# The token sum of phi(k) in a gated mix of linear attention and SwiGLU: from one matmul with ones to a transposing DMA, a DVE sum and a row in DRAM

## The chip, the cores and the metric

The kernel runs on one core of a Trainium2 chip. The metric is the device time of one execution in microseconds (us). The engines of the core work side by side, each through its own list of instructions in order: PE (TensorE) does matmuls, DVE (VectorE), ACT (ScalarE) and POOL (GpSimd) do elementwise work and sums, and SP (SyncE) issues the transfers (DMAs). An instruction that needs a result of another engine or of a transfer waits for it, and everything behind it on its own engine waits too.

## The reference, cut to what matters

```python
def A(x, wqkv, wo):                      # S = 2048 tokens, D = 512, H = 32 heads of 16
    q, k, v = split(x @ wqkv)
    phi = lambda t: jnp.where(t > 0, t + 1, jnp.exp(t)) + 1e-6
    pq, pk = phi(q), phi(k)
    kv = einsum("bhsd,bhse->bhde", pk, v)
    z = einsum("bhsd->bhd", pk)          # the token sum of phi(k)
    num = einsum("bhqd,bhde->bhqe", pq, kv)
    den = einsum("bhqd,bhd->bhq", pq, z)[..., None] + 1e-6
    return (num / den) @ wo
def B(x, w1, w3, w2):                    # F = 1376
    return (silu(x @ w1) * (x @ w3)) @ w2
g = sigmoid((x * gate_w).sum(-1))
out = g * A(x) + (1 - g) * B(x)
```

The sum `z` has 512 numbers, 16 for each head. Every token needs all of them for its 32 denominators.

## The kernel before, in words

The 2048 tokens are 16 tiles of 128 (index `t`), or 4 blocks of 512 (index `tb`). The order of the instructions on each engine is the order in which the Python program writes them.

The **first part**, to about 46 us, loops over the 16 tiles. `q_step` and `k_step` project a tile (L167) and form phi on ACT and DVE (L180 to L185). `g_step` (L215) gathers the product of x and phi(k) in four PSUM banks. At the end of each `k_step`, POOL adds phi(k) into `zacc` (L199); the last tile's addition writes `zaccb` in bf16. `zaccb` then holds, in each of the 128 partitions, a partial sum for each of the 512 features. One matmul with a matrix of ones (L376) sums over the partitions and leaves the result in all 128 partitions at once, and DVE copies it to `zb` (L377).

The **second part** loops over the four blocks. For each of the ten slices `fc` of F, `glu_step` does four matmuls for the gate (L262), four for the up half (L268), silu on ACT (L273) and the product on DVE into `hT` (L274). The four PSUM banks of these are taken in turn by `mm_tile`, also by `rem_step`. In the first block, `kv_step` follows at fc 2, `m2_step` (L404 and L406 copy `M2`) at fc 4 and `rem_step(0)` at fc 7. `rem_step` computes the last 96 columns of F and the gate, and issues a transposing DMA (L252) that writes the eleventh slice of `hT`. After the ten slices, `out_step` does one output tile at a time: four matmuls with the weights `pqT` (L414), then eleven with the weights `hT` (L427), the last of which uses the slice that L252 brought.

The denominators go beside this, tile by tile. `den_products` multiplies pq by `zb` on POOL (`pr`, L281). `den_sums` sums the heads on DVE, adds 1e-6 and takes the reciprocal (L285, L288, L292). `den_scale` multiplies pq by it on POOL (`pqs`, L296) and issues a transposing DMA to `pqT` (L301). `den_step(t)` is `den_sums(t)`, `den_products(t + 1)` and `den_scale(t)`. Tiles 0 to 3 are done in the first block, at the slices that `den_at` names; the other twelve follow output tiles.

All transfers but one small load are issued by SP in the program's order. First come the loads; after them, as the work goes, the transposes to `pqT` and `hT` and the output writes.

Of the kernel before, what the change touches and what calls it, by code (L numbers as in the profile page):

```python
# [8 lines left out]
ACT = mybir.ActivationFunctionType  # L9
ALU = mybir.AluOpType  # L10
AX = mybir.AxisListType
FP32 = mybir.dt.float32
BF16 = mybir.dt.bfloat16
# [3 lines left out]
def kernel(  # L17
# [17 lines left out]
    nc = tc.nc  # L35
    P = nc.NUM_PARTITIONS

    Bb, S, D = A_x.shape
# [3 lines left out]
    KC = D // P  # L42
# [4 lines left out]
    FC = F // P  # L47
# [10 lines left out]
    w1_r = B_w1.rearrange("(kc d) f -> d kc f", d=P)  # L58
    w3_r = B_w3.rearrange("(kc d) f -> d kc f", d=P)

    consts = ctx.enter_context(tc.tile_pool(name="consts", bufs=1))
    work = ctx.enter_context(tc.tile_pool(name="work", bufs=2))
    psum = ctx.enter_context(tc.tile_pool(name="psum", bufs=1, space=bass.MemoryType.PSUM))
    ctx.enter_context(tc.manual_schedule())

    warm = nc.const_aps.tensor(1.0, [P, 256], BF16)
# [1 line left out]
    make_identity(nc, ident[:])  # L68


    ones = consts.tile([P, P], BF16, name="ones")
    nc.gpsimd.memset(ones[:], 1.0)
    bmask = consts.tile([P, HPC, Dh], BF16, name="bmask")
    nc.gpsimd.memset(bmask[:], 1.0)
    nc.gpsimd.affine_select(
        out=bmask[:], in_=bmask[:], pattern=[[-Dh, HPC], [0, Dh]], compare_op=ALU.is_ge,
# [3 lines left out]
        out=bmask[:], in_=bmask[:], pattern=[[Dh, HPC], [0, Dh]], compare_op=ALU.is_ge,  # L80
# [5 lines left out]
    zacc = consts.tile([P, D], FP32, name="zacc")  # L86
    zaccb = consts.tile([P, D], BF16, name="zaccb")
    zb = consts.tile([P, D], BF16, name="zb")

# [9 lines left out]
    w1 = consts.tile([P, KC, F0], BF16, name="w1")  # L101
    w3 = consts.tile([P, KC, F0], BF16, name="w3")
    w2 = consts.tile([P, FC + 1, D], BF16, name="w2")
    xT = consts.tile([P, KC, S], BF16, name="xT")
    act_pre = consts.tile([P, 1], BF16, name="act_pre")
    dq = nc.sync
# [5 lines left out]
    def load_wqk(kc):  # L112
        dq.dma_start(out=wqk[:, kc, :], in_=wqkv_r[:, kc, 0 : 2 * D])
# [6 lines left out]
    nc.scalar.dma_start(out=touch[:], in_=wqkv_r[:, 1:3, 0:16])  # L120
    for kc in range(KC):
        load_wqk(kc)
    natural = {3: (2, 4), 5: (4, 8), 7: (8, 12), 11: (12, 16)}
    for t in range(2, NT):
        load_xT(t)
        if t in natural:
# [2 lines left out]
    with nc.allow_non_contiguous_dma(reason="gate column"):  # L129
        dq.dma_start(  # L130
            out=wr[:, :, 2 * FR : NR], in_=gate_w.rearrange("(kc d o) -> d kc o", d=P, o=1)
        )
    dq.dma_start(out=wr[:, :, 0:FR], in_=w1_r[:, :, F0:F])
    dq.dma_start(out=wr[:, :, FR : 2 * FR], in_=w3_r[:, :, F0:F])
    for w, w_r, cuts in ((w1, w1_r, (0, KC)), (w3, w3_r, (0, 2, KC))):
        for a, b in zip(cuts, cuts[1:]):
            dq.dma_start(out=w[:, a:b, :], in_=w_r[:, a:b, 0:F0])
    dq.dma_start(out=wv[:], in_=wqkv_r[:, :, 2 * D : 3 * D])
    dq.dma_start(out=wo[:], in_=A_wo.rearrange("(kc d) n -> d kc n", d=P))
    w2_r = B_w2[0:F0, :].rearrange("(fc f) d -> f fc d", f=P)  # L140
    for a, b in ((0, 5), (5, FC)):
        dq.dma_start(out=w2[:, a:b, :], in_=w2_r[:, a:b, :])
    dq.dma_start(out=w2[:FR, FC, :], in_=B_w2[F0:F, :])

    pq = consts.tile([P, NT, D], BF16, name="pq")
# [11 lines left out]
    def mm_tile():  # L157
        turn["mm"] += 1
        return bank[4 + (turn["mm"] - 1) % 4]

    def ab_tile():
        turn["ab"] += 1
        return bank[(turn["ab"] - 1) % 4]
# [49 lines left out]
    def g_step(t, kcs=range(KC)):  # L213
        for kc in kcs:
            nc.tensor.matmul(  # L215
                bank[kc][:], lhsT=xN[:, t, kc * P : (kc + 1) * P], rhs=pk[t][:],
                start=(t == 0), stop=(t == NT - 1),
            )


    def rem_step(tb):

        hr = hrem[tb % 2]
        for half in range(2):
            ps = mm_tile()[:].rearrange("p (j n) -> p j n", j=2)
            for j in range(2):
                t = tb * TPB + half * 2 + j
                for kc in range(KC):
                    nc.tensor.matmul(  # L229
                        ps[:, j, 0:NR], lhsT=xT[:, kc, t * P : (t + 1) * P],  # L230
                        rhs=wr[:, kc, 0:NR], start=(kc == 0), stop=(kc == KC - 1),
                    )
            t0 = tb * TPB + half * 2
            sg = work.tile([P, 2, FR], BF16, tag="sgr", name="sgr")
            nc.scalar.activation(out=sg[:], in_=ps[:, :, 0:FR], func=ACT.Silu)
            nc.scalar.activation(
                out=th_all[:, t0 : t0 + 2], in_=ps[:, :, 2 * FR], func=ACT.Tanh, scale=0.5
            )
            nc.vector.tensor_tensor(
                out=hr[:, half * 2 : half * 2 + 2, 0:FR], in0=ps[:, :, FR : 2 * FR],  # L240
                in1=sg[:], op=ALU.mult,
            )
        tl = slice(tb * TPB, (tb + 1) * TPB)
        nc.vector.tensor_scalar(
            out=g_all[:, tl], in0=th_all[:, tl], scalar1=0.5, scalar2=0.5,
            op0=ALU.mult, op1=ALU.add,
        )
        nc.vector.tensor_scalar(
            out=omg_all[:, tl], in0=th_all[:, tl], scalar1=-0.5, scalar2=0.5,
            op0=ALU.mult, op1=ALU.add,  # L250
        )
        dq.dma_start(  # L252
            out=hT[tb][:, FC, :].rearrange("p (tt q) -> p tt q", q=P),
            in_=hr[:].rearrange("p tt f -> p (tt f)"), transpose=True,
        )

    def glu_step(tb, fc):
        fs = slice(fc * P, (fc + 1) * P)
        tok = slice(tb * TB, (tb + 1) * TB)
        g_ps = mm_tile()  # L260
        for kc in range(KC):
            nc.tensor.matmul(  # L262
                g_ps[:], lhsT=w1[:, kc, fs], rhs=xT[:, kc, tok],
                start=(kc == 0), stop=(kc == KC - 1),
            )
        u_ps = mm_tile()
        for kc in range(KC):
            nc.tensor.matmul(  # L268
                u_ps[:], lhsT=w3[:, kc, fs], rhs=xT[:, kc, tok],
                start=(kc == 0), stop=(kc == KC - 1),  # L270
            )
        sg = work.tile([P, TB], BF16, tag="sg", bufs=3, name="sg")
        nc.scalar.activation(out=sg[:], in_=g_ps[:], func=ACT.Silu)  # L273
        nc.vector.tensor_tensor(out=hT[tb][:, fc, :], in0=u_ps[:], in1=sg[:], op=ALU.mult)  # L274
# [4 lines left out]
    def den_products(t):  # L279
        pr[t] = work.tile([P, D], FP32, tag="pr", bufs=3, name="pr")  # L280
        nc.gpsimd.tensor_tensor(out=pr[t][:], in0=pq[:, t, :], in1=zb[:], op=ALU.mult)  # L281
# [21 lines left out]
    def den_step(t):  # L303

        den_sums(t)
        if t + 1 < NT:
            den_products(t + 1)
        den_scale(t)
# [61 lines left out]
    for t in range(2, NT):  # L370
# [1 line left out]
        if t + 2 < NT:  # L372
            k_step(t + 2)
        g_step(t)
    z_ps = mm_tile()
    nc.tensor.matmul(z_ps[:], lhsT=ones[:], rhs=zaccb[:], start=True, stop=True)  # L376
    nc.vector.tensor_copy(out=zb[:], in_=z_ps[:])  # L377
    for kc in range(KC):
        if kc % 2 == 0:
            nc.vector.tensor_copy(out=Gsb[:, kc, :], in_=bank[kc][:])  # L380
# [3 lines left out]
    def kv_step():  # L384
        kv_ps = ab_tile()[:].rearrange("p (c q) -> p c q", q=P)
        for c in range(KC):
            cs = slice(c * P, (c + 1) * P)
            for kc in range(KC):
                nc.tensor.matmul(  # L389
                    kv_ps[:, c, :], lhsT=wv[:, kc, cs], rhs=Gsb[:, kc, cs],  # L390
                    start=(kc == 0), stop=(kc == KC - 1),
                )
        nc.vector.tensor_tensor(
            out=kvT[:], in0=kv_ps,
            in1=bmask[:].rearrange("p h d -> p (h d)")[:, None, :].to_broadcast([P, KC, P]),
            op=ALU.mult,
        )

    def m2_step():
        for c in range(KC):  # L400
            ps = ab_tile()
            nc.tensor.matmul(ps[:], lhsT=kvT[:, c, :], rhs=wo[:, c, :], start=True, stop=True)  # L402
            if c % 2 == 0:
                nc.scalar.activation(out=M2[:, c, :], in_=ps[:], func=ACT.Copy)  # L404
            else:
                nc.vector.tensor_copy(out=M2[:, c, :], in_=ps[:])  # L406
# [36 lines left out]
                cs = slice(2 * P, D)  # L443
            dq.dma_start(out=rows[:, cs], in_=o[:, cs])

    den_products(0)
    den_at = {0: 0, 1: 1, 3: 2, 6: 3}
    for tb in range(NTB):
        for fc in range(FC):
            glu_step(tb, fc)  # L450
            if tb == 0:
                if fc in den_at:
                    den_step(den_at[fc])
                if fc == 2:
                    kv_step()
                if fc == 4:
                    m2_step()
                if fc == 7:
                    rem_step(0)
        for tt in range(TPB):  # L460
            out_step(tb, tt)
            if tb + 1 < NTB:
                if tt == 0:
                    hT[tb + 1] = work.tile([P, FC + 1, TB], BF16, tag="hT", name="hT")
                if tt == 1:
                    rem_step(tb + 1)
                den_step((tb + 1) * TPB + tt)
# [30 lines left out]
```

## Time and profile before

| | |
|---|---|
| median of 3 runs | 179.43 us (179.19 to 179.78) |
| the profiled execution | 179.22 us, its span 177.5 us |
| PE busy | 173.9 us (98%), 880 matmuls |
| DVE, ACT, POOL busy | 100.5, 62.3, 62.9 us |
| granted PE clock | 1.00 |
| transfers | 15.15 MB in 28940 packets |

The span is the time from the first to the last instruction that the profile shows. "SPq" rows are transfers as SP issues them; a transfer lands later than its row ends. "PEld" is the loading of a matmul's weights, which goes on beside the matmul before it. In the timeline a row stands for one instruction or for several alike (x4), with its start and its length in us; what stands in brackets is how long the engine was idle before it, and what ended that.

### The profile page before, as it was taken

What the parts mean: (1) busy time and instruction counts of PE and PEld (TensorE: products, weight loads), DVE (VectorE), ACT (ScalarE), POOL (GpSimd) and SP (SyncE); (2) the same over time, 40 slices, a digit from 0 to 9 for tenths busy, and PEclk for the clock granted to TensorE, in tenths of its full rate; (3) what the DMA queues carried; (4) which work ended last, traced back from release to release, by engine and by line L of the source; (5) the groups of instructions that cost most, each with busy time, mean ns of one, the idle gap of its engine ahead of it and who ended that gap; (6) DMA issues with size and microseconds to landing.
All of it is one profiled execution on the core that took longest, in us unless ns stands there. A gap on an engine that the chain in (4) does not pass through costs nothing.

```text
span 177.5 us, 2504 instructions
## 1 busy us (share of the span) xinstructions
PE 173.9 (98%) x880; PEld 84.1 (47%) x880; DVE 100.5 (57%) x195; ACT 62.3 (35%) x113; POOL 62.9 (35%) x105
## 2 busy tenths in 40 slices
PE   8999999999999999999999999999999999999993
PEld 5444444444454464644444464444445444444453
DVE  1399788888899663575434166634325664433222
ACT  3354544444735441332342223142322223342130
POOL 5086656656577240446200044540004432000000
PEclk9999999999999999999999999999999999999999
DMA  5989869994002120233100013520000342000001
GB/s 174 269 202 216 163 106 264 406 381 142 4 0 59 30 47 16 59 82 96 30 0 4 0 40 80 90 63 0 0 0 30 89 92 59 0 0 0 30 33 59
DMA packets 28940, 15.15 MB, mean 85 GB/s; under 512 B 20896, under 2 KB 27264, under 8 KB 28928
## 3 DMA queue, kind: packets, MB, share of 16 engines
q1 hardware_dynamic: 28656, 14.98, 32.3%
q8 instruction: 7, 0.11, 0.3%
q14 instruction: 5, 0.04, 0.1%
q10 hardware_dynamic: 272, 0.01, 0.1%
HBM read 8.43 MB, written 2.10 MB: 59 GB/s over the span
## 4 chain that ended last, share of the span: by engine, by line
PE 98%; DVE 0%; issue 0%
PE bank L427 21%; PE bank L262 19%; PE bank L268 19%; PE bank L167 16%; PE bank L414 8%; PE bank L215 8%; PE bank L229 3%; PE bank L315 2%; PE bank L389 1%; PE bank L402 0%; PE bank L321 0%; DVE o L431 0%; PE bank L376 0%
## 5 line engine op out<-in xcount | busy, mean ns | idle before, releaser
L274 DVE TENSOR_TENSOR hT<-bank,sg 128x512 bf16<-128x512 f32 x40 | 27.2, 681 | 30.9 <-PE bank L268 30.9
L268 PE MATMUL bank<-xT,w 128*128 128x512 bf16 x160 | 41.1, 379 | 0.0
L262 PE MATMUL bank<-xT,w 128*128 128x512 bf16 x160 | 41.1, 379 | 0.0
L427 PE MATMUL bank<-w,hT 128*128 128x512 bf16 (+3 forms) x198 | 40.7, 355 | 0.0
L273 ACT ACTIVATE sg<-bank 128x512 bf16<-128x512 f32 x40 | 23.9, 597 | 46.9 <-PE bank L262 46.9
L296 POOL TENSOR_TENSOR pqs<-pq,rden 128x512 bf16<-128x512 bf16 x16 | 16.9, 1055 | 65.1 <-issue 60.0
L167 PE MATMUL bank<-wqk,xT 128*128 128x512 bf16 x128 | 30.6, 382 | 0.0
L431 DVE SCALAR_TENSOR_TENSOR o<-bank,omg_all,aga 128x512 bf16<-128x512 f32 (+2 forms) x18 | 12.5, 692 | 28.1 <-PE bank L427 28.0
L427 PEld LDWEIGHTS <-hT 128*128 128x128 bf16 (+1 forms) x198 | 18.5, 98 | 19.8
L199 POOL TENSOR_TENSOR zacc<-zacc,pk 128x128 f32<-128x128 f32 x56 | 23.3, 446 | 10.4 <-DVE pk L185 10.4
L268 PEld LDWEIGHTS <-w 128*128 128x128 bf16 x160 | 15.7, 98 | 18.9
L262 PEld LDWEIGHTS <-w 128*128 128x128 bf16 x160 | 15.6, 98 | 18.5
L419 ACT ACTIVATE aga<-bank,g_all 128x512 f32<-128x512 f32 x16 | 11.0, 687 | 28.9 <-PE bank L414 28.9
L167 PEld LDWEIGHTS <-xT 128*128 128x128 bf16 x128 | 12.5, 98 | 15.0 <-issue 0.5
L281 POOL TENSOR_TENSOR pr<-pq,zb 128x512 f32<-128x512 bf16 x16 | 18.4, 1153 | 1.7 <-DVE zb L377 1.7
L414 PE MATMUL bank<-M,pqT 128*128 128x512 bf16 x64 | 16.4, 378 | 0.0
L215 PE MATMUL bank<-pk,xN 128*128 128x512 bf16 x64 | 16.4, 379 | 0.0
L180 ACT ACTIVATE eq<-bank 128x512 bf16<-128x512 f32 x16 | 9.4, 597 | 16.0 <-PE bank L167 16.0
L185 DVE SCALAR_TENSOR_TENSOR pk<-bank,emk 128x512 bf16<-128x512 f32 x16 | 11.1, 692 | 1.6
L180 ACT ACTIVATE ek<-bank 128x512 bf16<-128x512 f32 x16 | 9.4, 597 | 6.6 <-PE bank L167 6.6
L185 DVE SCALAR_TENSOR_TENSOR pq<-bank,emq 128x512 bf16<-128x512 f32 x16 | 11.1, 692 | 0.6
L285 DVE TENSOR_REDUCE den<-pr 128x32 f32<-128x512 f32 x16 | 10.8, 676 | 0.0
(50 smaller groups left out, 81.7 us busy)
## 6 DMA issues: line engine op xcount, KB each, us to landing
w<-in_B_w_dram SPq DMA_DIRECT2D x4, 640.0 KB, 9.6
out_dram<-o SPq DMA_DIRECT2D x15, 128.0 KB, 1.9
xN<-in_A_x_dram SPq DMA_DIRECT2D x3, 512.0 KB, 4.5
w<-in_B_w_dram SPq DMA_DIRECT2D x1, 1280.0 KB, 7.6
wqk<-in_A_wqkv_dram SPq DMA_DIRECT2D x4, 256.0 KB, 3.7
xN<-in_A_x_dram SPq DMA_DIRECT2D x2, 256.0 KB, 2.9
wv<-in_A_wqkv_dram SPq DMA_DIRECT2D x1, 512.0 KB, 10.7
wo<-in_A_wo_dram SPq DMA_DIRECT2D x1, 512.0 KB, 11.1
```

The lines of the kernel that those rows point to most:

```text
L167: nc.tensor.matmul(ps[:], lhsT=xT[:, kc, t * P : (t + 1) * P], rhs=w[:, kc, :], start=(kc == 0), stop=(kc == KC - 1),)
L180: nc.scalar.activation(out=e[:], in_=ps[:], func=ACT.Exp)
L185: nc.vector.scalar_tensor_tensor(out=dst, in0=ps[:], scalar=0.0, in1=em[:], op0=ALU.max, op1=ALU.add)
L199: nc.gpsimd.tensor_tensor(out=(zaccb if t == NT - 1 else zacc)[:, cs], in0=zacc[:, cs], in1=pk[t][:, cs], op=ALU.add,)
L215: nc.tensor.matmul(bank[kc][:], lhsT=xN[:, t, kc * P : (kc + 1) * P], rhs=pk[t][:], start=(t == 0), stop=(t == NT - 1),)
L262: nc.tensor.matmul(g_ps[:], lhsT=w1[:, kc, fs], rhs=xT[:, kc, tok], start=(kc == 0), stop=(kc == KC - 1),)
L268: nc.tensor.matmul(u_ps[:], lhsT=w3[:, kc, fs], rhs=xT[:, kc, tok], start=(kc == 0), stop=(kc == KC - 1),)
L273: nc.scalar.activation(out=sg[:], in_=g_ps[:], func=ACT.Silu)
L274: nc.vector.tensor_tensor(out=hT[tb][:, fc, :], in0=u_ps[:], in1=sg[:], op=ALU.mult)
L281: nc.gpsimd.tensor_tensor(out=pr[t][:], in0=pq[:, t, :], in1=zb[:], op=ALU.mult)
L414: nc.tensor.matmul(a_ps[:], lhsT=pqT[:, c, ts], rhs=M2[:, c, :], start=(c == 0), stop=(c == KC - 1),)
L427: nc.tensor.matmul(b_ps[:, 0:w], lhsT=hT[tb][:n, fc, tl], rhs=w2[:n, fc, cs], start=(fc == 0), stop=(fc == FC),)
```

## The change

The matmul with ones, the memset of `ones` and the DVE copy to `zb` go. In their place:

- a transposing DMA turns `zaccb` into `zaT` (feature chunks in the partitions, tokens along the row),
- `z_step` sums along the row on DVE (512 elements to 4 in each partition), casts to bf16, writes the 512 numbers to a row in DRAM (`zrow`) in 128 pieces of 8 bytes, and reads that row back into all 128 partitions (`zpk`),
- `z_order` puts the features of `zpk` into their right order on ACT and writes `zb`. It stands behind the two ACT copies of `m2_step` at fc 4, and the first `den_products` stands behind it,
- the den steps of tiles 0 to 3 move from the slices 0, 1, 3, 6 to the slices 5, 6, 7, 8,
- three loads are merged with their neighbours: tokens 8 to 15 of `xN`, `w3`, and `w2`.

At fc 7 the den step of tile 2 now stands in front of `rem_step(0)`. The instruction lists show these moves and no others; on PE the only instructions that differ are the weight load and the matmul of L376.

```diff
-    ones = consts.tile([P, P], BF16, name="ones")
-    nc.gpsimd.memset(ones[:], 1.0)
+    zpk = consts.tile([P, D], BF16, name="zpk")
+    zaT = consts.tile([P, KC, P], BF16, name="zaT")
+    zTb = consts.tile([P, KC], BF16, name="zTb")
+    zrow = dram.tile([1, D], BF16, name="zrow")
...
-    natural = {3: (2, 4), 5: (4, 8), 7: (8, 12), 11: (12, 16)}
+    natural = {3: (2, 4), 5: (4, 8), 8: (8, 16)}
...
-    for w, w_r, cuts in ((w1, w1_r, (0, KC)), (w3, w3_r, (0, 2, KC))):
+    for w, w_r, cuts in ((w1, w1_r, (0, KC)), (w3, w3_r, (0, KC))):
...
-    for a, b in ((0, 5), (5, FC)):
-        dq.dma_start(out=w2[:, a:b, :], in_=w2_r[:, a:b, :])
+    dq.dma_start(out=w2[:, 0:FC, :], in_=w2_r)
...
-    z_ps = mm_tile()
-    nc.tensor.matmul(z_ps[:], lhsT=ones[:], rhs=zaccb[:], start=True, stop=True)
-    nc.vector.tensor_copy(out=zb[:], in_=z_ps[:])
+    dq.dma_start(out=zaT[:], in_=zaccb[:], transpose=True)
+
+    def z_step():
+        zT = work.tile([P, KC], FP32, tag="zT", bufs=1, name="zT")
+        nc.vector.tensor_reduce(out=zT[:], in_=zaT[:], op=ALU.add, axis=AX.X)
+        nc.vector.tensor_copy(out=zTb[:], in_=zT[:])
+        dq.dma_start(out=zrow[0, :].rearrange("(p kc) -> p kc", kc=KC), in_=zTb[:])
+        dq.dma_start(out=zpk[:], in_=zrow[0:1, :].to_broadcast([P, D]))
+
+    def z_order():
+        nc.scalar.activation(
+            out=zb[:].rearrange("p (kc q) -> p kc q", q=P),
+            in_=zpk[:].rearrange("p (q kc) -> p kc q", kc=KC), func=ACT.Copy,
+        )
...
-    den_products(0)
-    den_at = {0: 0, 1: 1, 3: 2, 6: 3}
+    z_step()
+    den_at = {5: 0, 6: 1, 7: 2, 8: 3}
...
                 if fc == 4:
                     m2_step()
+                    z_order()
+                    den_products(0)
                 if fc == 7:
                     rem_step(0)
```

More of the change, by code (lines that the diff above doesn't have):

```diff
@@ L63 @@
     psum = ctx.enter_context(tc.tile_pool(name="psum", bufs=1, space=bass.MemoryType.PSUM))
+    dram = ctx.enter_context(tc.tile_pool(name="dram", bufs=1, space=bass.MemoryType.DRAM))
     ctx.enter_context(tc.manual_schedule())
```

## The prediction, made before the changed kernel had run

> **What bounds the kernel now.** I read the page from the top: busy shares, then the chain that ended last.
>
> ```profile
> PE 173.9 (98%) x880; PEld 84.1 (47%) x880; DVE 100.5 (57%) x195; ACT 62.3 (35%) x113; POOL 62.9 (35%) x105
> ...
> PE 98%; DVE 0%; issue 0%
> ```
>
> PE is busy from end to end and carries 98% of the chain; only the time before its first matmul and after its last one is not PE. So a saving counts only if it takes matmuls off PE, and an addition costs only if PE comes to wait for it. DVE, ACT and POOL have room on average; what matters is when their results arrive.
>
> Next the chain cut to the place of the change, start and duration in us:
>
> ```profile
> 45.53 0.86 PE bank L215 x4
> 46.39 0.24 PE bank L376
> 46.63 0.86 PE bank L262 x4
> 47.49 0.86 PE bank L268 x4
> ```
>
> L376 is the token sum of phi(k), one matmul with a slot of 0.24 us. PE does not stand still for it: the last piece of `zaccb` ends on POOL at 44.50 + 1.70 = 46.20, before the slot begins. Afterwards the glu groups (L262 gate, L268 up) follow each other every 0.86 us.
>
> Then the timeline, for what the four early den steps do today and what comes next on each engine (start, duration, engine, line, operation):
>
> ```profile
> 44.50 1.70 POOL L199 TENSOR_TENSOR zaccb<-zacc,pk 128x128 bf16<-128x128 f32 x4 [1.12 <-DVE pk L185]
> ...
> 47.13 0.68 DVE L377 CAST zb<-bank 128x512 bf16<-128x512 f32 x1
> ...
> 47.89 2.27 POOL L281 TENSOR_TENSOR pr<-pq,zb 128x512 f32<-128x512 bf16 x2 [1.69 <-DVE zb L377]
> ...
> 49.08 0.69 DVE L274 TENSOR_TENSOR hT<-bank,sg 128x512 bf16<-128x512 f32 x1
> ...
> 56.41 1.09 ACT L404 ACTIVATE M<-bank 128x512 bf16<-128x512 f32 x2 [0.48 <-PE bank L402]
> ...
> 58.86 0.69 DVE L274 TENSOR_TENSOR hT<-bank,sg 128x512 bf16<-128x512 f32 x1 [0.54 <-PE bank L268]
> ...
> 64.97 1.22 SPq L252 DMA_TRANSPOSE hT<-hrem  x1
> ...
> 67.47 2.26 PEld L427 LDWEIGHTS <-hT 128*128 128x128 bf16 x11
> ```
>
> The last two rows are the ones that decide. L252 moves the remainder block of `hT`; it is issued at 64.97 and lands 2.4 us later, at 67.4. It is the weights of the eleventh L427 matmul of the first output tile. The eleven weight loads begin at 67.47, one each 0.216 us, so the eleventh begins at 67.47 + 10 x 0.216 = 69.63: 2.2 us of room before the change.
>
> **What is removed.** The matmul: 0.24 us of PE, all of it on the path. Everything after it on PE, where nothing else is late, moves 0.24 earlier; I subtract that below. The `zb` cast (0.68 on DVE) goes too, off the path. So does the memset of `ones` on POOL, at the start, where POOL waits 5.7 us for the first pk. With `z_ps` gone the four glu banks turn by one place: the second gate-up pair now uses banks of q(14) and q(15), the latter freed by DVE at 46.52 + 0.69 = 47.21 and wanted at about 48.8. No cost.
>
> **The merged loads.** Tokens 8 to 15 of xN come in one 1 MB transfer, the w3 and w2 loads become one each. The bytes are the same. xT(9) is the first with more ahead of it, 512 KB; at the 202 to 269 GB/s of the second and third slice that is 2.0 to 2.6 us. It is issued near 14.0, landed within 4.8 us at worst, and its k projection runs at 25.7, so the cover is 6.9 us; without it the cost would be up to those 2.6 us on PE. The w2 load is needed at 67 and the traffic of all loads ends near 41, before and after. Zero, from 0 to +0.2.
>
> **The new chain to `zpk`.** The transposing DMA follows `zaccb` on SP, whose loads are all issued by 38: issue 46.22. The SBUF-to-SBUF transposes (pqT, L301) land in 2.4 us at the median and 3.2 at the worst, so 48.62. DVE has by then ended the two Gsb casts (47.21 + 1.28 = 48.5). The 512-element reduce costs the 0.68 of the den reduce, the 128x4 cast 0.16 (row of omg_all): done at about 49.5. Behind these two on DVE stands the first hT multiply (49.08 before); it now runs 49.54 to 50.23. Who waits for that is the third up group, which reuses its bank: 50.78 - 0.24 = 50.54. So the wait is hidden with 0.3 us to spare; a landing of 3.2 would cost 0.5. The next hT starts earlier than before, since the den sums are no longer between.
>
> The row write of 128 pieces of 8 bytes has no equal in the trace. Above stands the gate column (1 KB in 2-byte pieces) at 2.8 and the touch load (32-byte pieces) at 2.9; below the 64 KB output write at 1.5; the worst output write is 3.7. I take 2.9, the small-piece rows being nearest. The read by all partitions, 1 KB each: from 2.6 (the 96 KB wr loads) to 4.8 (worst xN); I take 2.8. Issued at 49.6, that makes 52.5 and 55.3. SP waits twice, and behind it stand only the pqT transposes, which have nothing to move yet.
>
> The Trainium skill's page "DMA: Bandwidth & Descriptors" (Specifications) speaks against this step: transfers under 512 bytes are done by read-modify-write. Its section "Anatomy of one DMA", a fit for another issuing path, puts 2.0 us plus bytes over 436 GB/s on each, which as an estimate makes 2.0 and 2.3 us and ends the chain at 53.9 in place of 55.3; the sum would be the same by both, as the next step does not start before 57.
>
> **ACT copy and the late den steps.** `z_order` stands on ACT behind the two M2 copies: 57.50 - 0.24 = 57.26. So the chain above has 2.0 us of cover. I give the copy 0.60 (ACT rows of 128x512: 0.54 to 0.69), to 57.86. The sg activation behind it (57.92 - 0.24 = 57.68 before) starts 0.2 late, and its hT multiply, which waits for PE until 58.62, does not notice.
>
> From here the order is POOL: pr0, pr1, scale0, pr2, scale1, pr3, scale2. pr0 and pr1 take 2.27, from 57.94 to 60.21. DVE does hT(5) to 58.86 + 0.69 - 0.24 = 59.31, then sums0: 1.28 (reduce start to reciprocal end, as at 61.19 to 62.47), to 60.59; 0.09 on to POOL. Now POOL is the limit: scale0 1.06, pr2 1.15, scale1 1.06, pr3 1.15, scale2 1.06 from 60.68: 5.48, to 66.16. DVE's sums1 and sums2 (about 62.4 and 64.2) are ready before POOL asks.
>
> SP then issues pqT(2) at 66.18, and only behind it the hT remainder, since `den_step` stands ahead of `rem_step` at fc 7: 1.28 us later (63.69 to 64.97 in the trace), 67.46. It lands 2.4 us on, at 69.86. PE wants it at 69.63 - 0.24 = 69.39. So PE waits 0.47 us in the first output tile. Before the change this room was 2.2 us; it is used up by moving four den steps behind the glu steps that follow M2.
>
> Other readers: pqT(0) lands at about 64.2 for 66.4, pqT(1) at 66.4 for 69.6, pqT(2) at 68.6 for 74.3, pqT(3) at 71 for 77.4. The first remainder multiply on DVE goes from 63.33 to behind sums2 and ends near 64.7 (hT(6), sums1, hT(7), sums2 one after another); the bank that it frees is asked for at 65.10 - 0.24 = 64.86, so 0.1 to 0.2 us of cover, and a wait there would put off PE's need of the hT remainder by as much, so the two do not add. From the fourth output tile on all is as before.
>
> **The sum.** -0.24 + 0.47 = +0.23 us. The profiled execution took 179.22 (span 177.5 and 1.7 around it), so 179.45; the median of the runs is 0.21 above the profiled one, so 179.6 (179.66, of which I take the lower side, since a weight load of 98 ns has a slot of 216 and so some 0.1 us in hand). A measurement of this kernel can tell about 0.3%, 0.54 us, from no change. So: no measurable change.
>
> **Rivals.**
> - *Nothing is late.* If the POOL chain is half a microsecond quicker, or the reduce is, PE keeps the whole 0.24: 179.2. For it: many of these rows overlap by 0.03 to 0.1. Against: seven steps in series have to give it. Also inside 0.3%. A gain above 0.54 has no place in the chain, as no more PE work leaves; it would need a shift in the kernel's start or end that I can't see.
> - *Slower: the trip through DRAM decides.* ACT waits for `zpk` with M2 done. This begins when the read lands after 57.26, that is when write and read take over 7.6 us together. With the worst rows, 3.7 + 4.8, it lands at 58.1, 0.84 late; 0.14 is hidden under hT(5) and 0.7 goes one for one into the hT remainder: +0.9, 180.35. Each microsecond more costs one more. For it: piece size and the write-then-read pair are outside the trace. Against: even 2-byte pieces under full load took 2.8.
> - *Slower: the first hT is late.* The transposing DMA lands at 3.2 instead of 2.4: third up group 0.5 late, +0.7, 180.15. Against: 15 of 16 pqT landings are 2.4 or 2.5.
> - *The change does less than it says:* the merged loads delay a projection before 46 us, up to +2.6 with the cover gone. Against: 6.9 us of cover.
>
> **How the numbers follow.** My sum with its stall between nothing and 0.75 (so a net of -0.24 to +0.5, the first rival included): 0.65, all within 0.3%. The DRAM trip or a POOL chain longer than I have it: 0.18; the late first hT: 0.08; loads: 0.04; together 0.30 slower. Faster by over 0.3%: 0.05, unexplained. The range runs from 179.0 (first rival less the scatter of the runs, 0.2) to 180.6 (DRAM rival plus the same); what is left out is a DRAM trip over 8.8 us, delayed loads and an unexplained gain.
>
> **What would show it.** Right: no L376 on PE; zaT landing near 48.6, zpk by 56; ACT's copy starting near 57.3 behind M2 and not behind a DMA; hT remainder issued near 67.5; the idle time of PE's eleventh L427 weight load in the first output tile at 0.2 to 0.6 us, released by the hT DMA. Wrong: idle time on ACT before the copy, on PE at the third L268 group, or before 46 us.

## The result and the profile after

| | before | changed |
|---|---|---|
| median | 179.44 us (179.12 to 179.78, 6 runs) | 181.05 us (180.68 to 181.28, 6 runs) |
| ratio, 95% interval | | 1.0079 (1.0063 to 1.0095) |
| profiled execution | 179.22 us, span 177.5 | 180.97 us, span 179.3 |

The changed kernel is slower by 0.8%, 1.1 to 1.7 us by the interval. The page of the changed kernel shows PE at the same work (one weight load fewer; 16 of its matmul records are missing) and the chain no longer on PE alone:

```profile
PE 173.4 (97%) x863; PEld 84.1 (47%) x879; DVE 101.7 (57%) x196; ACT 62.6 (35%) x114; POOL 62.8 (35%) x104
...
PE 93%; DVE 4%; issue 1%; DVEq 0%
```

The 4% of DVE lie almost all in one place, from 59 to 67 us. This is the chain of the changed kernel at the end of it (start, duration, what):

```profile
64.29 0.60 DVE den L287
...
64.92 1.12 DVE den L290
...
66.33 0.30 DVE hrem L241
66.64 0.04 issue
66.68 1.02 PE bank L264 x4
```

The timeline there, with POOL beside DVE. In `den_sums`, L287 is the sum over the heads, L290 the addition of 1e-6 (128x32) and L294 the reciprocal; on POOL, L283 is the product of `den_products` and L298 the scaling of `den_scale`; L241 is the remainder multiply in `rem_step`, L246 a step of the gate behind it:

```profile
58.39 2.26 POOL L283 TENSOR_TENSOR pr<-pq,zb 128x512 f32<-128x512 bf16 x2 [11.70 <-ACT zb L389]
...
60.44 0.25 DVE L290 TENSOR_SCALAR den<-den 128x32 f32<-128x32 f32 x1
...
61.54 0.67 DVE L287 TENSOR_REDUCE den<-pr 128x32 f32<-128x512 f32 x1
...
62.17 1.15 POOL L283 TENSOR_TENSOR pr<-pq,zb 128x512 f32<-128x512 bf16 x1
...
62.25 1.11 DVE L290 TENSOR_SCALAR den<-den 128x32 f32<-128x32 f32 x1
...
63.40 0.35 DVE L294 RECIPROCAL rden<-den 128x32 f32<-128x32 f32 x1
...
64.84 1.15 POOL L283 TENSOR_TENSOR pr<-pq,zb 128x512 f32<-128x512 bf16 x1
64.92 1.11 DVE L290 TENSOR_SCALAR den<-den 128x32 f32<-128x32 f32 x1
...
66.33 0.56 DVE L241 TENSOR_TENSOR hrem<-bank,sgr 128x192 bf16<-128x192 f32 x2
66.50 1.05 POOL L298 TENSOR_TENSOR pqs<-pq,rden 128x512 bf16<-128x512 bf16 x1 [0.51 <-DVE rden L294]
66.68 1.02 PE L264 MATMUL bank<-xT,w 128*128 128x512 bf16 x4 [1.16 <-DVE hrem L241]
...
66.81 0.77 DVE L246 TENSOR_SCALAR g_all<-th_all 128x4 f32<-128x4 f32 x1
...
68.87 0.18 DVE L290 TENSOR_SCALAR den<-den 128x32 f32<-128x32 f32 x1
```

An addition that takes 0.18 us alone takes 1.11 when a product of POOL has just begun, and ends 0.04 us after the product. This happens in tiles 1 and 2, so the remainder multiply (L241) runs late, the PSUM bank that it frees is late, and the first gate matmul of fc 9 waits for it: 1.54 us from the matmul before it in place of 0.22. In the kernel before, the same group starts without a wait:

```profile
65.10 1.03 PE L262 MATMUL bank<-xT,w 128*128 128x512 bf16 x4
```

The hold lasts as long as what is left of POOL's instruction. Tile 0's addition met the last 0.2 us of its two products (58.39 + 2.26 = 60.65) and took 0.25; L246, of the same form (TENSOR_SCALAR), met a scaling and took 0.77. All four end 0.03 to 0.04 us after POOL's instruction.

The profiled execution is 1.75 us longer. Three terms are read from the two timelines. The first is the start: the first gate weights of fc 0 are loaded at 46.52 in place of 46.26, although the matmul of 0.24 us in front of them is gone, so the part up to there took 0.50 longer. The second is the stretch from there to the end of the last matmul: 129.77 in place of 128.46, +1.31. The third is the end, from the last matmul to the end of the span: 2.96 in place of 2.78, +0.18.

### The profile page after: what moved, and what is told of

Same layout as the page of the kernel before. It is cut to its first block, busy times and chain, and to the rows that moved or that the text cites. A ratio compares the mean times of both kernels' runs of the same rounds, so it can differ in the third digit from the quotient of the medians.

```text
span 179.3 us, 2489 instructions
## 1 busy us (share of the span) xinstructions
PE 173.4 (97%) x863; PEld 84.1 (47%) x879; DVE 101.7 (57%) x196; ACT 62.6 (35%) x114; POOL 62.8 (35%) x104
## 4 chain that ended last, share of the span: by engine, by line
PE 93%; DVE 4%; issue 1%; DVEq 0%
PE bank L443 21%; PE bank L264 18%; PE bank L270 17%; PE bank L169 16%; PE bank L217 8%; PE bank L430 8%; PE bank L231 2%; PE bank L317 2%; DVE den L290 1%; DVE hT L276 1%; DVE den L287 1%; PE bank L405 0%; PE bank L418 0%; PE bank L323 0%; DVE o L447 0%
## 5 line engine op out<-in xcount | busy, mean ns | idle before, releaser
L264 PE MATMUL bank<-xT,w 128*128 128x512 bf16 x158 | 40.9, 379 | 1.4 <-DVE hrem L241 1.2
L443 PE MATMUL bank<-w,hT 128*128 128x512 bf16 (+4 forms) x197 | 40.6, 355 | 0.1
L270 PE MATMUL bank<-xT,w 128*128 128x512 bf16 x154 | 40.3, 379 | 0.2
L298 POOL TENSOR_TENSOR pqs<-pq,rden 128x512 bf16<-128x512 bf16 x16 | 16.9, 1055 | 56.1 <-issue 50.8
L283 POOL TENSOR_TENSOR pr<-pq,zb 128x512 f32<-128x512 bf16 x16 | 18.4, 1153 | 11.7 <-ACT zb L389 11.7
L287 DVE TENSOR_REDUCE den<-pr 128x32 f32<-128x512 f32 x16 | 10.8, 676 | 0.0
```

Of the source, the lines that this page charges most:

```text
L264: nc.tensor.matmul(g_ps[:], lhsT=w1[:, kc, fs], rhs=xT[:, kc, tok], start=(kc == 0), stop=(kc == KC - 1),)
L270: nc.tensor.matmul(u_ps[:], lhsT=w3[:, kc, fs], rhs=xT[:, kc, tok], start=(kc == 0), stop=(kc == KC - 1),)
L443: nc.tensor.matmul(b_ps[:, 0:w], lhsT=hT[tb][:n, fc, tl], rhs=w2[:n, fc, cs], start=(fc == 0), stop=(fc == FC),)
```

## The experiments

Theory 1: the addition stands still beside POOL, makes the bank late, and PE waits. Theory 2: the den steps are late in themselves, through the trip to DRAM or the chain of products on POOL. "Stretch" and "end" below are the second and third term above, from each kernel's profile, to about 0.01 us; ratios are to the kernel before, run on the same chip. The rows come from several chips, so two medians alone do not compare.

| | median us | ratio (95%) | fc 0 weights at | stretch | end |
|---|---|---|---|---|---|
| before (profile of 179.22) | 179.44 | | 46.26 | 128.46 | 2.78 |
| changed | 181.05 | 1.0079 (1.0063 to 1.0095) | 46.52 | 129.77 | 2.96 |
| e1 changed again | 181.01 | 1.0077 (1.0063 to 1.0092) | 46.57 | 129.78 | 2.97 |
| e2 no add | 179.45 | 1.0004 (0.9989 to 1.0018) | 46.64 | 128.46 | 2.99 |
| e3 remainder first | 179.67 | 0.9999 (0.9984 to 1.0015) | 46.76 | 128.46 | 2.99 |
| e4 late den alone | 180.98 | 1.0071 (1.0051 to 1.0091) | 46.55 | 129.71 | 2.77 |
| e5 reduce for add | 179.65 | 0.9991 (0.9972 to 1.0009) | 46.94 | 128.56 | 2.97 |
| e6 extra ACT | 180.06 | 1.0013 (0.9995 to 1.0032) | 46.94 | 128.46 | 2.97 |
| e7 merged loads alone | 179.63 | 0.9997 (0.9980 to 1.0015) | 46.52 | 128.47 | 2.98 |
| e8 remainder first, POOL copy | 179.51 | 0.9974 (0.9955 to 0.9993) | 46.55 | 128.46 | 2.79 |
| e11 tiles 2, 3 at fc 8, 9, POOL copy | 179.19 | 0.9986 (0.9971 to 1.0001) | 45.92 | 128.46 | 2.78 |
| e12 before, no add | 179.67 | 1.0011 (0.9994 to 1.0028) | 46.70 | 128.46 | 2.79 |

**e1, the changed kernel again.** No edit.

> The changed kernel unaltered, in another call. Two things made up the +1.75 us of its profile: PE waits 1.3 us for a bank at the ninth slice's successor (gate matmuls of fc 9), and everything before 46 us is 0.5 us late because the PE clock was granted at 5.97 us of the span in place of 5.00. If the grant falls by chance, this run's profile has another grant time and the front moves with it, half a us per us, and the middle (fc 9) still has its 1.3 us. If the merged loads or the new tiles cause the late front, the grant is again near 5.9 to 6.0 and the time 181.0.

The time and the wait at fc 9 came back (1.53 us between matmuls). The start was late again, but not as I had it: the clock record begins with full grant at 4.94 us, 1.03 earlier than in the first profile, and the first gate weights still came at 46.57. Here the slow first matmuls are short, 1.26 us for four, and PE instead lost about half a microsecond waiting at 6.8 and 7.5 us, which is when the third and fourth wqk loads landed (issued near 2.2 and 2.7, 4.6 and 4.8 us under way). So the start varies for at least two reasons. This run alone does not show that the change has no part in it; the kernels of e4, e6, e7 and e12, which keep the old token sum, have the first gate weights at 46.52 to 46.94.

**e2, without the addition.**

```diff
-        nc.vector.tensor_scalar(out=den[:], in0=den[:], scalar1=1e-6, scalar2=None, op0=ALU.add)
```

> Leaves out the addition of 1e-6 in den_sums (all 16 tiles). Theory 1 (that addition, a DVE tensor_scalar, stands still while a POOL product runs: 1.11 us in place of 0.18 for tiles 1 and 2, which makes the remainder multiply late and with it the bank of fc 9): den sums take 1.0 to 1.1 us, PE's wait at fc 9 is gone, the hT remainder may then be waited for by up to 0.47 us; 0.9 to 1.3 us less than the changed kernel, 179.8 to 180.2. Theory 2 (the den steps are too late in themselves, POOL's chain of products sets the end): POOL's chain is as long as before, at most 0.3 us less, 180.7 to 181.0.

The stretch is that of the kernel before to 0.01 us, and the time falls 1.6. Theory 2 said 0.3 at most. The late hT remainder shows in the weight loads of this run, where the eleventh waits for its transfer:

```profile
68.08 1.82 PEld L440 LDWEIGHTS <-hT 128*128 128x128 bf16 x9
70.09 0.10 PEld L440 LDWEIGHTS <-hT 96*128 96x128 bf16 x1 [0.19 <-DMA hT<-hrem]
70.24 0.75 PEld L427 LDWEIGHTS <-pqT 128*128 128x128 bf16 x4
```

The loads behind it are back in step at 70.24: PE lost nothing.

**e3, remainder first.**

```diff
+                if fc == 7:
+                    rem_step(0)
                 if fc in den_at:
                     den_step(den_at[fc])
...
-                if fc == 7:
-                    rem_step(0)
```

> The changed kernel with rem_step(0) ahead of den_step(2) at fc 7. Theory 1: the remainder multiplies run before sums2, the bank of fc 9 is free in time and the hT remainder is issued near 65; the collisions stay and now delay hT(8) and hT(9): hT(9) ends near 69.9, 0.2 us after PE wants its weights. 0.8 to 1.2 us less than the changed kernel, 179.9 to 180.3. Theory 2 (the chain through DRAM and POOL is what PE waits for): no difference, 181.0.

The direction is theory 1's, the size was missed: PE has no wait at all. The additions are as slow as before in tiles 1 and 3 (1.11; tile 2's took 0.43), and hT(9) ends at 69.87, when its weights are asked for near 69.9.

**e4, the late den steps alone**, with the matmul for the token sum and without any of the new transfers.

```diff
-    den_products(0)
-    den_at = {0: 0, 1: 1, 3: 2, 6: 3}
+    den_at = {5: 0, 6: 1, 7: 2, 8: 3}
...
                     m2_step()
+                    den_products(0)
```

> The kernel before, with its matmul for the token sum and its loads, but den_products(0) behind m2_step and den steps 0 to 3 at fc 5 to 8. Theory 1: the adds of tiles 1 and 2 collide with POOL's products as in the changed kernel, PE waits at fc 9 for 0.6 to 1.3 us: 180.1 to 180.8. Rival (the new chain with its transfers is the cause): 179.4, no wait of PE at fc 9.

This one edit costs what the whole change costs. Its timeline has the same two rows and the same wait, with `zb` ready since 48 us:

```profile
62.13 1.16 POOL L281 TENSOR_TENSOR pr<-pq,zb 128x512 f32<-128x512 bf16 x1
62.20 1.12 DVE L288 TENSOR_SCALAR den<-den 128x32 f32<-128x32 f32 x1
...
64.80 1.15 POOL L281 TENSOR_TENSOR pr<-pq,zb 128x512 f32<-128x512 bf16 x1
64.88 1.11 DVE L288 TENSOR_SCALAR den<-den 128x32 f32<-128x32 f32 x1
...
66.64 1.02 PE L262 MATMUL bank<-xT,w 128*128 128x512 bf16 x4 [1.09 <-DVE hrem L239]
```

**e5, another operation in the addition's place.**

```diff
-        nc.vector.tensor_scalar(out=den[:], in0=den[:], scalar1=1e-6, scalar2=None, op0=ALU.add)
+        den2 = work.tile([P, H], FP32, tag="den2", name="den2")
+        nc.vector.tensor_reduce(
+            out=den2[:], in_=den[:].rearrange("p (h d) -> p h d", d=1), op=ALU.add, axis=AX.X
+        )
...
-        nc.vector.reciprocal(out=rden[t][:], in_=den[:])
+        nc.vector.reciprocal(out=rden[t][:], in_=den2[:])
```

> The changed kernel with the addition of 1e-6 (left out) replaced by a DVE tensor_reduce over one element, of the same 128x32 size: as many DVE instructions and as much DVE work as in the changed kernel, but an operation whose rows never stretched beside POOL (den reduce 0.67 to 0.69 everywhere). Theory 1 (only the tensor_scalar form stands still beside POOL): the replacement takes about 0.2 us in tiles 1 and 2, PE's wait at fc 9 is 0 to 0.4 us, 179.5 to 179.9. Rival (any third DVE instruction there, or a wait of it for the reduce's result, takes 1.1 us): as the changed kernel, 181.0.

The replacement (L291) takes 0.18 and 0.19 in tiles 1 and 2 with an instruction of POOL in flight, a product and a scaling:

```profile
62.60 0.18 DVE L291 TENSOR_REDUCE den<-den 128x32 f32<-128x32 f32 x1
...
64.44 0.19 DVE L291 TENSOR_REDUCE den<-den 128x32 f32<-128x32 f32 x1
```

```profile
62.53 1.15 POOL L283 TENSOR_TENSOR pr<-pq,zb 128x512 f32<-128x512 bf16 x1
63.64 1.06 POOL L299 TENSOR_TENSOR pqs<-pq,rden 128x512 bf16<-128x512 bf16 x1
```

So it is the form of the instruction, and not a third DVE instruction at that place. The Trainium skill's page "SBUF — State Buffer" (Who interferes with whom) states this rule: a tensor_scalar on SBUF data may take the port pair that DVE shares with GpSimd, and then the later of the two waits until the other's instruction is over, while a tensor_reduce on trn2 never does. The rows agree with both halves: 1.11 us, ending 0.04 after the product, against 0.18. They show the wait and its end; that a port is what is held no run here shows.

**e6, one more ACT instruction in the kernel before.**

```diff
+    act_two = consts.tile([P, 1], BF16, name="act_two")
...
                     m2_step()
+                    nc.scalar.activation(out=act_two[:], in_=warm[:, 0:1], func=ACT.Copy)
```

> The kernel before with one more ACT instruction (a copy of one column, used by nothing) behind m2_step. In the changed kernel's profile, and in all three variants of it with the ACT copy, the ACT drain in the closing barrier comes 0.27 us later than in the kernel before, and the time from the last matmul to the span's end is 2.96 to 2.99 in place of 2.78. Theory A (the length of ACT's instruction list decides it): here too 2.96, and the time 179.6 to 179.7. Theory B (it belongs to the DRAM row or its transfers): 2.78 and 179.5.

The end is 2.97, as theory A has it. These are the two ACT drains at the close of the program (shortest, median and longest in ns) in the kernel before, the changed kernel, e6 and e8, in this order:

```profile
L493 ACTq DRAIN  x2: 14/366/717, 172.3 to 177.1; - x2
```

```profile
L511 ACTq DRAIN  x2: 141/429/717, 173.9 to 178.9; - x2
```

```profile
L495 ACTq DRAIN  x2: 141/430/719, 173.0 to 178.0; - x2
```

```profile
L511 ACTq DRAIN  x2: 14/368/721, 172.6 to 177.4; - x2
```

The closing one takes 141 ns in place of 14 and begins about 0.27 later, counted from the last matmul, in the two with one ACT instruction more. The time alone does not tell it: 0.13% slower, with an interval that includes no difference. It rests on the trace; why one more instruction does this stays open.

**e7, the merged loads alone.** Only the three load lines of the change, in the kernel before.

> The kernel before with the three merged loads alone. If they are hidden as predicted, the time is 179.5 within 0.15 and PE has no wait between 10 and 46 us. If they had part in the late front of the changed kernel (0.5 us in its profile), 179.7 to 180.0.

As predicted, no wait and no difference. Its end of 2.98 has another cause, as its closing ACT drain is short: with three transfers fewer, three of SP's closing waits follow the last landing instead of preceding it, 0.065 us each.

**e8, remainder first and the copy on POOL.**

```diff
-        nc.scalar.activation(out=zb[:]..., in_=zpk[:]..., func=ACT.Copy)
+        nc.gpsimd.tensor_copy(out=zb[:]..., in_=zpk[:]...)
```

> The changed kernel with rem_step(0) ahead of the den step at fc 7 and with the reordering copy on POOL in place of ACT (as many ACT instructions as the kernel before). No wait of PE at fc 9, as in the run with rem_step first; by theory A the end is 2.78 us again. What is left of the change is then its 0.24 us: 179.2 to 179.3, 0.2 below the kernel before. By theory B the end stays at 2.96: 179.4 to 179.5.

Faster than the kernel before, by 0.07 to 0.45% (the expected 0.24 us is 0.13%), and with the short end of 2.79 that theory A asks for.

**e9 and e10, the read by all partitions.**

```diff
-        dq.dma_start(out=zpk[:], in_=zrow[0:1, :].to_broadcast([P, D]))
+        dq.dma_start(out=zpk[:], in_=x2d[0:P, :])                          # e9
+        dq.dma_start(out=zpk[:], in_=x2d[0:1, :].to_broadcast([P, D]))     # e10
```

> The changed kernel with zpk read from 128 different rows of A_x, 1 KB to each partition, in place of the one row zrow: the right denominators are left out. The read of zrow landed 3.8 to 4.3 us after its issue in six profiles, where 2.8 had been taken. If the one row or its freshness is what makes it long, this read of as many bytes lands in 2.0 to 2.8 us; if any 128 KB read in 1 KB pieces takes that long here, 3.8 to 4.3.

> The changed kernel with zpk read from one row of A_x by all 128 partitions (the right denominators are left out): a row that no transfer of the kernel has written. If reading one row 128 times is what takes long, the read lands in 3.8 to 4.3 us; if it is that zrow was written just before, in 2.0 to 2.8 us.

Neither expectation came true: 5.7 us in e9 and 6.5 in e10, one execution each. Both reads were issued 0.41 us after the row write and so ran beside it, which the read of `zrow` does not. So the runs do not separate the single row or its freshness from the rest; they show only that a read of many rows, none of them just written, can be as long. What makes it long stays open.

**e11, tiles 2 and 3 one slice later**, with the copy on POOL, `rem_step(0)` left in its place.

```diff
-    den_at = {5: 0, 6: 1, 7: 2, 8: 3}
+    den_at = {5: 0, 6: 1, 8: 2, 9: 3}
```

> The changed kernel with the reordering copy on POOL and the den steps of tiles 2 and 3 at fc 8 and 9 in place of 7 and 8, so that rem_step(0) is in front of them. The adds may still stand still beside POOL (1.1 us), but only o(0) and hT(9) are behind them, and hT(9) ends near 69 where PE wants it near 69.7. No wait of PE at fc 9; 0.24 us less than the kernel before, which is 0.1%: its interval should reach from about -0.3% to +0.05%.

As expected, without a wait, though the additions of tiles 1 and 3 still take 1.11 us; the interval just includes no difference.

**e12, the kernel before without the addition.** The edit of e2.

> The kernel before without the addition of 1e-6 (left out). One of its adds also stands still beside POOL (52.14, 1.12 us), with nothing waiting for it. If the 1.5 us that leaving out the add gave in the changed kernel came from the wait at fc 9 and not from the add's own time, this makes no difference: 179.5 within 0.2. If the 16 adds cost time by themselves, 0.3 to 1.5 us less.

No difference. What e2 gained was the wait, not the addition's own time.

## Why the prediction was wrong

**The step that failed** is the one that took 1.28 us for the den sums of every tile and concluded that sums1 and sums2 "are ready before POOL asks". Tile 0's took 1.35; tiles 1 and 2 took 2.21 and 2.20, because their additions stood 1.11 us beside POOL's products, and POOL then waited 0.51 us for each. On the prediction's clock (0.50 us taken off for the late start) sums2 ended at 65.9 in place of 64.2, and the remainder multiply at 66.1 in place of 64.7. The next sentence had the rest right: the bank is asked for at 64.86, with 0.1 to 0.2 us of cover, and what exceeds it makes PE wait. It became 1.3 us.

The evidence was in the trace of before, in rows that I had not put side by side (52.14 is the addition of tile 1):

```profile
52.06 1.16 POOL L281 TENSOR_TENSOR pr<-pq,zb 128x512 f32<-128x512 bf16 x1
52.14 1.12 DVE L288 TENSOR_SCALAR den<-den 128x32 f32<-128x32 f32 x1
```

The 1.28 came from the sums of tile 3, where POOL stood idle:

```profile
61.19 0.68 DVE L285 TENSOR_REDUCE den<-pr 128x32 f32<-128x512 f32 x1
...
61.90 0.18 DVE L288 TENSOR_SCALAR den<-den 128x32 f32<-128x32 f32 x1
...
62.12 0.35 DVE L292 RECIPROCAL rden<-den 128x32 f32<-128x32 f32 x1
```

That one tile collides there and two do here is no chance: with den steps in neighbouring slices both engines start from the same reciprocal. POOL scales for 1.05 us and begins the next product; DVE multiplies hT (0.63) and reduces (0.67), so that its addition comes 0.08 us after that product has begun, in all three. e11 agrees, with den steps at 5, 6, 8 and 9: the additions of tiles 1 and 3 take 1.11 us, those of tiles 0 and 2 take 0.18.

**The rest of the chain** was right where the additions do not stand still. In e5 the sums of tiles 1 and 2 take 1.27 and 1.29 us, POOL works from the first scaling to the third without a wait, and the hT remainder is issued at 67.2 on the prediction's clock (67.46 forecast).

**The removed matmul**: 0.24 us off PE, right by the instruction lists; the times of e8 and e11, 0.26% and 0.14% below the kernel before, agree with it (0.13%), though the interval of e11 includes no difference. **The end**: not in the prediction; 0.18 us for the one ACT instruction more (e6). **The late hT remainder**, +0.47: over-sized. In e2 and e5, where nothing else is late, PE lost 0.0 and 0.1. In e5 the eleventh weights waited 0.41 us, about 0.3 more than the usual pause between two loads, and PE lost 0.1: some 0.2 us were absorbed.

**The sum** by the runs is -0.24 + 1.31 + 0.18 = +1.25 us, inside the measured 1.1 to 1.7. The other 0.50 of the profiled pair is the start. Over the twelve profiles of the table, the first gate weights come between 45.92 and 46.94, in kernels with and without the change (take 0.24 off where the matmul stands).

**The trip through DRAM** did not decide, as the prediction had it, but with less room. Landings in the changed kernel:

```profile
zpk<-zrow SPq DMA_DIRECT2D x1, 128.0 KB, 4.1
...
zrow<-zTb SPq DMA_DIRECT2D x1, 1.0 KB, 2.7
```

The write was sized right (2.9 taken), the read was not (2.8 taken); both came later than the 2.0 and 2.3 us of the prediction's second estimate. `zpk` was there at 56.9 and ACT began its copy at 57.64, behind M2: 0.7 us of cover in place of 2.0. The transposing DMA landed in 2.4, the reduce took 0.69, and the first hT multiply made nobody wait: right. So were the merged loads (e7). **The rivals**: none of the three that name a slower path came true; they put the risk into the transfers, and it lay in two engines that the change only moved against each other. "A POOL chain longer than I have it", which stands only among the chances, came nearest, but without the addition that made it longer.

## What to carry to other kernels

Price a moved instruction by the rows where its new neighbours run beside it, not by its quiet row: where one group has a mean of 240 ns and rows of 0.18 and 1.12, the spread is the finding. A tensor_scalar on SBUF operands in a chain with POOL products can cost the whole product, here 1.11 us for 0.18; a change of form (here a reduce) or of order (the work that frees a PSUM bank first) takes the cost away. And when a cover of 0.1 us is found under a sum of a dozen steps, it is the likeliest place for the loss and deserves a rival of its own.

## What the runs showed that I had not expected

- The closing ACT drain takes 127 to 142 ns in place of 14 and comes 0.26 to 0.31 us later with one more ACT instruction, in all six profiles of the table that have one; the end grows by about 0.2 us.
- The 128 pieces of 8 bytes were sent within 0.2 us, in 7 to 9 ns each; the row landed 2.7 to 3.2 us after its issue all the same, later than the 64 KB output writes (1.5).
- A read of 128 KB in 1 KB pieces, alone on the queue, landed in 3.8 to 4.3 us, and in 5.7 and 6.5 beside the small write, while the two 256 KB loads of `xN` in the kernel before landed in 2.7 and 3.1.
- In the ten traces that have a clock record, full grant begins between 3.8 and 6.6 us after the start, another time in each execution. In the changed kernel it begins at 5.97 us, and the four projection matmuls started before that take 0.53 to 0.63 us each and the later ones 0.38; the first four took 1.76 us together, and 1.30 in the kernel before (5.00).
